# Attention scores as 64-row by 32-column tiles of the array, with another order of the opening loads

## The chip, the core and the metric

The kernel runs on one core of one Trainium2 chip. The metric is the device time of one execution in microseconds (us). TensorE is called PE here, its weight loads PEld, VectorE DVE, ScalarE ACT, GpSimd POOL and SyncE SP, as the profile names them.

## The reference

Attention with RMS-normalised queries and keys over 8 batches, 12 heads, 448 positions and 64 dimensions a head, followed by a feed-forward part on the 3584 tokens: two products with 768 by 1024 weights, multiplied with each other, then two more products without anything in between.

```
q_n, k_n = rmsnorm(q, g_q), rmsnorm(k, g_k)        # x / sqrt(mean(x*x) + 1e-6) * g
scores = matmul(q_n, k_n^T) / sqrt(64)
attn = softmax(scores)
x = (attn @ v) as 3584 x 768
h = (x @ w1) * (x @ w2) @ w3
out = h @ w_out
```

## The kernel before

**Staging.** The 96 (batch, head) pairs are worked on as NQ = 24 groups of HQ = 4 heads. The loop at L473 runs over the groups (and one round more), with four slots each (`sl`); t = 4 i + sl numbers the slots. In one slot the kernel issues, in this order for PE: the scores of two key blocks of a head pair (`qk_exp`, L226), one set of the products with v for the group before (`pv_set`, L248: first the row sums with a matrix of ones, then the two halves of the head dimension), then either units of a weight product (slots 1 to 13) or up to two units of the feed-forward part (`fill`), and then what is due of the preparation of later groups. The order is written out by hand, and each engine works through its own instructions in this order.

**Scores.** 448 positions are four blocks of NP = 112. For one key block, `qk_exp` issues two matmuls, one for each head of the pair (L235): head u lies on partitions 64 u to 64 u + 63 of `qkT`, so each matmul uses 64 rows of the array and all 112 columns, and streams the 448 queries. Both land in one PSUM tile `sc` (two banks, two such tiles in turn), and one ACT instruction takes the exponential of both (L244). A slot has two key blocks, four matmuls.

**Other PE work.** `pv_set` (L259) and the feed-forward part (`narrow`, L314) issue groups of four matmuls of 32 columns each, at column positions 0, 32, 64 and 96, over all rows (112 and 128). In slots 1 to 13 the product w3 times w_out is made once, so that the feed-forward part needs three products and not four: `w3_transpose` (L293, transposes of 128 by 128) and `w34_unit` (L301, matmuls of 128 by 128 streaming 384 columns). `w34q` at L443 orders these units: the second half of the output columns (nh = 1) follows the first by LAG = 4 chunks, and `W34_SLOTS` says how many units a slot takes. From slot 14 on, feed-forward units take that place.

**Preparation.** For each group, squares on ACT (L157), sums on DVE (L166), the factor 1/rms as `alpha` on ACT (L176, L177), the scaling on DVE (`prep_scale`, L188 to L201, with the product of both g vectors, `g_b`), then the transposition of the scaled q and k to `qkT`: for the groups below N_PE_T = 5 on PE (L220) with a copy by DVE (L223), for the others by a transposing DMA on SP's queue (L210). The tables PREP and SHIFT say in which slot before its use each part is issued.

**Opening.** POOL's queue first broadcasts g_q and g_k to 112 partitions (L401, L402). q and k of group 0 are loaded in two parts each, q on SP's queue and k on ACT's, then q and k of group 1 on SP's. A small POOL copy (L410, `gate`) reads the last part of k and so holds back POOL's weight loads behind it: both pieces of w_out's first column half (`load_wout(0, ...)`), four chunks of w3, v of group 0, both pieces of w_out's second half. Sixteen matmuls on zeros (`warm`) run at the start. The remaining loads are in the list `wq` (L432), four of which are issued in each slot: w3 chunks 4 to 7, v of groups 1 and 2, then w1 and w2. At L424 and L425 DVE multiplies the two g vectors and the factor 8 into `g_b`, between `alpha` and the first scaling.

Of the kernel before, what the change touches and what calls it, by code (L numbers as in the profile page):

```python
# [8 lines left out]
FP = mybir.dt.float32  # L9
BF = mybir.dt.bfloat16  # L10
MULT = mybir.AluOpType.mult
# [7 lines left out]
def kernel(  # L19
# [13 lines left out]
    nc = tc.nc  # L33

    B, H, S, D = q.shape
    NP = 112
    J = S // NP
    HQ = 4
# [4 lines left out]
    CF = DFF // 128  # L43
# [4 lines left out]
    const = ctx.enter_context(tc.tile_pool(name="const", bufs=1))  # L48
# [9 lines left out]

    big_pool = ctx.enter_context(tc.tile_pool(name="big", bufs=2))

    N_PE_T = 5
    N_SQ_ACT = 24
    W34_EV = "DA"
    LAG = 4
    SHIFT = [0, 0, 0, -1, -2, -3, -4]
    PREP_1 = {
        "sq0": -4, "red0": -4, "sq1": -4, "red1": -3, "alpha": -3,
# [11 lines left out]
    w_outs = const.tile([128, CF, DM], BF, name="w_outs")  # L79
    w3s = big_pool.tile([128, CF, DFF], BF, tag="big", name="w3s")  # L80
    w3T = big_pool.tile([128, CF, DFF], BF, tag="big", name="w3T")
    gq_b = const.tile([NP, D], FP, name="gq_b")
    gk_b = const.tile([NP, D], FP, name="gk_b")
    g_b = const.tile([NP, D], BF, name="g_b")
    ident = const.tile([128, 128], BF, name="ident")
    ones = const.tile([NP, HALF], BF, name="ones")
# [11 lines left out]
    def load_qk(i, split=1, k_eng=None):  # L98
        b, m = divmod(i, NQB)
        s = st[i]  # L100
        s["q"] = load_pool.tile([NP, HQ, J, D], FP, tag="q", name="q_sb")
        s["k"] = load_pool.tile([NP, HQ, J, D], FP, tag="k", name="k_sb")
        n = HQ // split
        for h0 in range(0, HQ, n):
            for t_sb, src, eng in (
                (s["q"], q, nc.sync),
                (s["k"], k, k_eng or nc.sync),
            ):
                eng.dma_start(
                    out=t_sb[:, h0 : h0 + n].rearrange("p h j d -> p h (j d)"),  # L110
                    in_=src[b, HQ * m + h0 : HQ * m + h0 + n].rearrange(
                        "h (p j) d -> p h (j d)", j=J
                    ),
                )

    def load_v(i):
        b, m = divmod(i, NQB)
        s = st[i]
        s["v"] = load_pool.tile([NP, HQ, J, D], BF, tag="v", name="v_sb", bufs=4)
        nc.gpsimd.dma_start(  # L120
            out=s["v"].rearrange("p h j d -> p h (j d)"),
            in_=v[b, HQ * m : HQ * (m + 1)].rearrange("h (p j) d -> p h (j d)", j=J),
        )
# [9 lines left out]
    def load_w3(c):  # L133
        nc.gpsimd.dma_start(
            out=w3s[:, c, :],
            in_=moe_w3.rearrange("(c p) f -> p c f", p=128)[:, c, :],
        )

    def load_wout(nh, c):
        nc.gpsimd.dma_start(  # L140
            out=w_outs[:, 4 * c : 4 * c + 4, nh * NH : (nh + 1) * NH],
            in_=moe_w_out.rearrange("(c p) n -> p c n", p=128)[
                :, 4 * c : 4 * c + 4, nh * NH : (nh + 1) * NH
            ],
        )


    def prep_sq(i, pr, on_act=False):
# [77 lines left out]
    def qk_exp(i, g):  # L226
        s = st[i]
        if g == 0:
            s["P"] = att_pool.tile([NP, HQ, J, S], BF, tag="P", name="P")
        pr, t = divmod(g, 2)  # L230
        qkT, P = s["qkT"], s["P"]
        for jk in (2 * t, 2 * t + 1):
            sc = sc_psum.tile([NP, 2, 512], FP, tag="sc", name="sc")
            for u in range(2):
                nc.tensor.matmul(  # L235
                    out=sc[:, u, 0:S],
                    lhsT=qkT[u * D : (u + 1) * D, pr, J + jk, :],
                    rhs=qkT[u * D : (u + 1) * D, pr, 0:J, :].rearrange(
                        "d j p -> d (j p)"
                    ),  # L240
                    start=True,
                    stop=True,
                )
            nc.scalar.activation(  # L244
                out=P[:, 2 * pr : 2 * pr + 2, jk, :], in_=sc[:, :, 0:S], func=AF.Exp
            )
# [151 lines left out]

    with tc.manual_schedule():

        nc.gpsimd.dma_start(out=gq_b, in_=g_q.unsqueeze(0).broadcast_to([NP, D]))  # L401
        nc.gpsimd.dma_start(out=gk_b, in_=g_k.unsqueeze(0).broadcast_to([NP, D]))  # L402
        nc.vector.memset(warm_t, 0.0)
        nc.vector.memset(eps_t, 64e-6)
        nc.vector.memset(ones, 1.0)
        load_qk(0, split=2, k_eng=nc.scalar)
        nc.scalar.preload_act_table_set("natural_log_exp_and_others")
        load_qk(1)
        make_identity(nc, ident)
        nc.gpsimd.tensor_copy(out=gate, in_=st[0]["k"][:, HQ - 1, 0, 0:1])  # L410
        load_wout(0, 0)
        load_wout(0, 1)
        for c in range(4):
            load_w3(c)
        load_v(0)
        load_wout(1, 0)
        load_wout(1, 1)
        warm(16)
        for pr in range(2):
            prep_sq(0, pr, on_act=True)  # L420
            prep_red(0, pr)
            prep_alpha(0, 2 * pr, 2 * pr + 2)
            if pr == 0:
                nc.vector.tensor_tensor(out=gq_b, in0=gq_b, in1=gk_b, op=MULT)  # L424
                nc.vector.tensor_scalar(  # L425
                    out=g_b, in0=gq_b, scalar1=8.0, scalar2=None, op0=MULT
                )
            prep_scale(0, pr, pe=True)
            if pr == 0:
                prep_pe_transpose(0, 0)  # L430

        wq = [lambda c=c: load_w3(c) for c in range(4, CF)]  # L432
        wq.insert(2, lambda: load_v(1))
        wq.append(lambda: load_v(2))
        for h in range(HQ):
            for half in range(2):
                for w, src in ((w1s, moe_w1), (w2s, moe_w2)):
                    wq.append(
                        lambda w=w, src=src, h=h, half=half: load_w12(w, src, h, half)
                    )  # L440
        wq.append(lambda: load_v(3))

        w34q = [lambda: w3_transpose(0), lambda: w3_transpose(1)]  # L443
        for fc in range(CF + LAG):
            if fc < CF:
                w34q.append(lambda fc=fc: w34_unit(fc, 0))
            if fc + 2 < CF:
                w34q.append(lambda fc=fc: w3_transpose(fc + 2))
            if fc >= LAG:
                w34q.append(lambda fc=fc: w34_unit(fc - LAG, 1))  # L450

        def prep_part(n, part):
            pe = n < N_PE_T
            if part[:2] == "sq":
                prep_sq(n, int(part[2]), on_act=n < N_SQ_ACT)
            elif part[:3] == "red":
                prep_red(n, int(part[3]))
            elif part == "alpha":
                prep_alpha(n)
            elif part[:2] == "sc":  # L460
                prep_scale(n, int(part[2]), pe=pe)
            elif pe:
                prep_pe_transpose(n, int(part[1]))


        agenda = {}
        for n in range(1, NQ):
            shift = SHIFT[min(n, len(SHIFT)) - 1]
            table = PREP_1 if n == 1 else PREP
            for part, rel in table.items():  # L470
                agenda.setdefault(max(0, 4 * n + rel + shift), []).append((n, part))

        for i in range(NQ + 1):  # L473
            for sl in range(4):
                t = 4 * i + sl
                mine = agenda.pop(t, [])
                for n, part in mine:
                    if part == "load":
                        load_qk(n)
                if i < NQ:  # L480
                    qk_exp(i, sl)
                if t == 0:
                    prep_pe_transpose(0, 1)
                seen = len(fillers)
                if i > 0 and sl < 3:
                    pv_set(i - 1, sl)
                fresh = fillers[seen:]
                if sl == 0 and 4 <= i + 1 < NQ:
                    load_v(i + 1)
                for _ in range(4):  # L490
                    if wq:
                        wq.pop(0)()
                if t in W34_SLOTS:
                    for _ in range(W34_SLOTS[t]):
                        if w34q:
                            w34q.pop(0)()
                elif not w34q:
                    left = (14 - t) % 12 + 1
                    old = len(fillers) - sum(1 for f in fillers if f in fresh)
                    fill(min(2, -(-old // left)))  # L500
                for n, part in mine:
                    if part[0] == "t":
                        prep_part(n, part)
                for n, part in mine:
                    if part[0] != "t" and part != "load":
                        prep_part(n, part)
        fill(len(fillers))
# [28 lines left out]
```

## Time and profile before

Six runs: median 391.97 us, from 391.19 to 393.34.

| | us |
|---|---|
| the profiled execution | 391.9 |
| its span, first to last instruction | 390.0 |
| score matmuls, L235, busy (384 of them, mean 378 ns) | 57.4 |
| their exponentials on ACT, L244, busy (192, mean 916 ns) | 165.4 |
| feed-forward matmuls pa, pb, po, L314, busy | 84.0, 83.7, 77.9 |
| products with v and row sums, L259, busy | 45.1, 22.6 |
| weight product, L301, busy | 24.0 |
| PE transposes of q and k, L220, busy (80, 10 sets of 8) | 7.0 |
| DVE waits for g_k | 3.0 |
| transposing DMAs, L210: 38, us to landing, least / median / most | 2.9 / 4.1 / 6.3 |

Busy times of matmuls have modelled ends and overlap each other; a mean of 378 ns for a matmul is its way through the array, while the next one has already started. The mean granted clock of PE is 0.982 of the full one; over the span's stretch from 10 to 20 us it was 0.57, from 20 to 30 us 0.75, and 1.00 from 30 us on. In the stretches from 10 to 60 us the DMA engines were busy all the time (a share above 1, as packets overlap); from 70 to 80 us the share was 0.49.

The first feed-forward matmul starts at 68.9 us, the last load of w1 and w2 was issued at 53.0, and the last stretch, from 356 us on, has feed-forward work alone.

### The profile page before, as it was taken

What the parts mean: (1) busy time and instruction counts of PE and PEld (TensorE: products, weight loads), DVE (VectorE), ACT (ScalarE), POOL (GpSimd) and SP (SyncE); (2) the same over time, 40 slices, a digit from 0 to 9 for tenths busy, and PEclk for the clock granted to TensorE, in tenths of its full rate; (3) what the DMA queues carried; (4) which work ended last, traced back from release to release, by engine and by line L of the source; (5) the groups of instructions that cost most, each with busy time, mean ns of one, the idle gap of its engine ahead of it and who ended that gap; (6) DMA issues with size and microseconds to landing.
All of it is one profiled execution on the core that took longest, in us unless ns stands there. A gap on an engine that the chain in (4) does not pass through costs nothing.

```text
span 390.0 us, 14802 instructions
## 1 busy us (share of the span) xinstructions
PE 372.7 (96%) x6688; PEld 193.1 (50%) x6688; DVE 242.4 (62%) x383; ACT 285.3 (73%) x467; POOL 35.4 (9%) x61
## 2 busy tenths in 40 slices
PE   5498999999999999999999999999999999999995
PEld 1154554544544455445544554445445555456563
DVE  1775766887767677567766766757776672234232
ACT  4568889998888885897898768888889857751210
POOL 5332440000000000000000000000000000000000
PEclk9579999999999999999999999999999999999999
DMA  8999999387895589675877489559854651003014
GB/s 188 229 238 237 207 227 188 61 156 140 200 206 87 117 167 211 121 164 92 192 173 155 78 222 208 73 110 198 207 91 122 119 141 27 3 12 114 2 26 140
DMA packets 78367, 55.08 MB, mean 141 GB/s; under 512 B 37824, under 2 KB 72160, under 8 KB 78304
## 3 DMA queue, kind: packets, MB, share of 16 engines
q1 hardware_dynamic: 61568, 41.30, 44.8%
q0 software_dynamic: 16256, 12.38, 22.6%
q8 instruction: 52, 0.85, 1.0%
q10 hardware_dynamic: 480, 0.46, 0.4%
q14 instruction: 11, 0.09, 0.1%
HBM read 46.72 MB, written 11.01 MB: 148 GB/s over the span
## 4 chain that ended last, share of the span: by engine, by line
PE 87%; DMA 8%; ACT 1%; DVE 1%; POOL 0%; issue 0%; ACTq 0%
PE pa L314 19%; PE po L314 19%; PE pb L314 19%; PE pv L259 15%; PE sc L235 12%; DMA w3s<-in_moe_w_dram 4%; PE wps L301 3%; DMA w_outs<-in_moe_w_out_dram 3%; DMA k_sb<-in_k_dram 1%; PE w3T_ps L293 1%; PE qkT_ps L220 0%; ACT P L244 0%; DVE qtmp L188 0%; ACT w34s L286 0%; DVE qks L201 0%; ACT sq L157 0%
## 5 line engine op out<-in xcount | busy, mean ns | idle before, releaser
L244 ACT ACTIVATE P<-sc 112x896 bf16<-112x896 f32 x192 | 165.4, 916 | 41.7 <-PE sc L235 41.7
L344 DVE TENSOR_TENSOR abT<-pb,a_sb 128x448 bf16<-128x448 f32 x64 | 40.0, 625 | 77.0 <-PE pb L314 56.6
L314 PE MATMUL pa<-xT,w1s 128*32 128x448 bf16 x1536 | 84.0, 353 | 0.0
L314 PE MATMUL pb<-xT,w2s 128*32 128x448 bf16 x1536 | 83.7, 352 | 0.0
L314 PE MATMUL po<-w34s,abT 128*32 128x384 bf16 x1792 | 77.9, 326 | 0.0
L166 DVE TENSOR_REDUCE ssq<-sq 112x16 f32<-112x1024 f32 x48 | 58.3, 1215 | 13.9 <-ACT sq L157 13.9
L314 PEld LDWEIGHTS <-abT 128*32 128x32 bf16 x1792 | 47.2, 97 | 27.7 <-issue 2.4
L235 PE MATMUL sc<-qkT 64*112 64x448 bf16 x384 | 57.4, 378 | 0.7 <-DVE qkT L223 0.7
L314 PEld LDWEIGHTS <-w2s 128*32 128x32 bf16 x1536 | 41.1, 97 | 31.5
L314 PEld LDWEIGHTS <-w1s 128*32 128x32 bf16 x1536 | 39.7, 96 | 34.1 <-issue 4.7
L331 ACT CAST a_sb<-pa 128x448 bf16<-128x448 f32 x64 | 34.0, 531 | 26.5 <-PE pa L314 26.5
L363 DVE COPY o_sb<-po 128x384 f32<-128x384 f32 x56 | 31.2, 557 | 31.5 <-PE po L314 31.5
L259 PE MATMUL pv<-P,v_sb 112*32 112x448 bf16 x768 | 45.1, 355 | 0.0
L120 POOL DMA_DIRECT2D v_sb<-in_v_dram x24 | 17.0, 708 | 238.2 <-PE pv L259 217.8
L188 DVE TENSOR_TENSOR qtmp<-q_sb,alpha 112x512 bf16<-112x512 f32 x48 | 32.8, 683 | 6.8 <-ACT alpha L177 6.8
L235 PEld LDWEIGHTS <-qkT 64*112 64x112 bf16 x384 | 17.4, 126 | 31.8 <-issue 29.4
L201 DVE TENSOR_TENSOR qks<-k_sb,alpha 112x512 bf16<-112x512 f32 x48 | 32.9, 685 | 0.0
L275 DVE TENSOR_TENSOR xT<-pv,r 128x448 bf16<-128x448 f32 x48 | 29.6, 618 | 3.2 <-PE pv L259 3.2
L157 ACT ACTIVATE sq<-q_sb 112x512 f32<-112x512 f32 x48 | 30.4, 634 | 1.5 <-DMA q_sb<-in_q_dram 1.5
L157 ACT ACTIVATE sq<-k_sb 112x512 f32<-112x512 f32 x48 | 30.0, 625 | 0.0
L259 PEld LDWEIGHTS <-v_sb 112*32 112x32 bf16 x768 | 16.2, 95 | 23.7 <-issue 15.6
L301 PE MATMUL wps<-w_outs,w3T 128*128 128x384 bf16 x128 | 24.0, 338 | 0.0
(36 smaller groups left out, 174.3 us busy)
## 6 DMA issues: line engine op xcount, KB each, us to landing
q_sb<-in_q_dram SPq DMA_DIRECT2D x23, 448.0 KB, 5.5
k_sb<-in_k_dram SPq DMA_DIRECT2D x23, 448.0 KB, 6.1
v_sb<-in_v_dram POOLq DMA_DIRECT2D x24, 224.0 KB, 4.8
out_dram<-o_sb SPq DMA_DIRECT2D x8, 336.0 KB, 3.9
out_dram<-o_sb SPq DMA_DIRECT2D x8, 288.0 KB, 3.6
w3s<-in_moe_w_dram POOLq DMA_DIRECT2D x8, 256.0 KB, 15.6
out_dram<-o_sb SPq DMA_DIRECT2D x8, 240.0 KB, 4.0
w_outs<-in_moe_w_out_dram POOLq DMA_DIRECT2D x4, 384.0 KB, 13.5
```

The source lines that it names most:

```text
L157: nc.scalar.activation(out=sq[:, t], in_=src[:, hs], func=AF.Square)
L166: nc.vector.tensor_reduce(out=s["ssq"][:, :, hs, :], in_=s.pop(("sq", pr)), axis=AX, op=ADD)
L188: nc.vector.tensor_tensor(out=qtmp.transpose([0, 2, 1, 3]), in0=s["q"][:, hs], in1=alpha[:, 0, hs].unsqueeze(3).broadcast_to([NP, 2, J, D] ...
L201: nc.vector.tensor_tensor(out=qks[:, 1].transpose([0, 2, 1, 3]), in0=s["k"][:, hs], in1=alpha[:, 1, hs].unsqueeze(3).broadcast_to([NP, 2, ...
L235: nc.tensor.matmul(out=sc[:, u, 0:S], lhsT=qkT[u * D : (u + 1) * D, pr, J + jk, :], rhs=qkT[u * D : (u + 1) * D, pr, 0:J, :].rearrange("d ...
L244: nc.scalar.activation(out=P[:, 2 * pr : 2 * pr + 2, jk, :], in_=sc[:, :, 0:S], func=AF.Exp)
L259: nc.tensor.matmul(out=ps[h * HALF : (h + 1) * HALF, :], lhsT=w, rhs=P[:, h, jk, :], start=(jk == 0), stop=(jk == J - 1), tile_position=(0 ...
L301: nc.tensor.matmul(out=ps[:, 0:NH], lhsT=w3T[:, gc, fc * 128 : (fc + 1) * 128], rhs=w_outs[:, gc, nh * NH : (nh + 1) * NH], start=(gc == 0 ...
L314: nc.tensor.matmul(out=ps[32 * h : 32 * h + 32, 0:n], lhsT=lhsT[:, 32 * h : 32 * h + 32], rhs=rhs, start=start, stop=stop, tile_position=( ...
L331: nc.scalar.copy(out=a_sb, in_=ps[:, 0:S])
L344: nc.vector.tensor_tensor(out=abT[bp][:, fi, odd * S : (odd + 1) * S], in0=ps[:, 0:S], in1=a_tiles.pop((b, fi)), op=MULT,)
L363: nc.vector.tensor_copy(out=o_sb[:, nh * NH : (nh + 1) * NH], in_=ps[:, 0:NH])
```

## The change

Each score matmul of 64 rows by 112 columns becomes four of 64 rows by 32 columns (the last one has 16), at row position 64 u and column position c0. A key block of a head pair is then eight matmuls, at eight different places of the array, which stream the same queries and write the same PSUM tile in strips of 32 partitions.

The opening is reordered. The g vectors are no longer broadcast by POOL's DMAs: each is loaded as one row of 64 on ACT's queue, behind the k loads; DVE multiplies both rows and the factor 8 into `gp_row` on one partition, one matmul with a row of ones spreads it over 112 partitions, and DVE copies that from PSUM to `g_b`. The `gate` copy now reads the first part of q and not the last part of k. POOL's loads follow in the order of LOADS_0 and then LOADS_1: w3 chunk 4 and v of group 0 come earlier, w_out's second half comes later. LAG is 8 and not 4, so the units of w_out's second half all follow those of the first. N_PE_T is 3 and not 5: groups 3 and 4 are transposed by DMA. QK1_AT = -1 leaves the load of group 1 where it was.

```diff
-    N_PE_T = 5
+    N_PE_T = 3
-    LAG = 4
+    LAG = 8
+    LOADS_0 = ["o0", "w0", "w1", "w2", "v0", "w3", "w4"]
+    LOADS_1 = ["w5", "v1", "w6", "w7", "o1", "v2"]
+    GATE = ("q", 0)
+    QK1_AT = -1
...
+    def load_any(x):
+        kind, a = x[0], int(x[1])
+        if kind == "o":
+            load_wout(a, 0)
+            load_wout(a, 1)
+        elif kind == "w":
+            load_w3(a)
+        else:
+            load_v(a)
...
             for u in range(2):
-                nc.tensor.matmul(
-                    out=sc[:, u, 0:S],
-                    lhsT=qkT[u * D : (u + 1) * D, pr, J + jk, :],
-                    rhs=qkT[u * D : (u + 1) * D, pr, 0:J, :].rearrange(
-                        "d j p -> d (j p)"
-                    ),
-                    start=True,
-                    stop=True,
-                )
+                for c0 in range(0, NP, 32):
+                    c1 = min(c0 + 32, NP)
+                    nc.tensor.matmul(
+                        out=sc[c0:c1, u, 0:S],
+                        lhsT=qkT[u * D : (u + 1) * D, pr, J + jk, c0:c1],
+                        rhs=qkT[u * D : (u + 1) * D, pr, 0:J, :].rearrange(
+                            "d j p -> d (j p)"
+                        ),
+                        start=True,
+                        stop=True,
+                        tile_position=(u * D, c0),
+                    )
...
-        nc.gpsimd.dma_start(out=gq_b, in_=g_q.unsqueeze(0).broadcast_to([NP, D]))
-        nc.gpsimd.dma_start(out=gk_b, in_=g_k.unsqueeze(0).broadcast_to([NP, D]))
...
+        nc.vector.memset(ones_row, 1.0)
         load_qk(0, split=2, k_eng=nc.scalar)
+        nc.scalar.dma_start(out=g_row[:, 0], in_=g_q.unsqueeze(0))
+        nc.scalar.dma_start(out=g_row[:, 1], in_=g_k.unsqueeze(0))
         nc.scalar.preload_act_table_set("natural_log_exp_and_others")
-        load_qk(1)
+        if QK1_AT < 0:
+            load_qk(1)
         make_identity(nc, ident)
-        nc.gpsimd.tensor_copy(out=gate, in_=st[0]["k"][:, HQ - 1, 0, 0:1])
-        load_wout(0, 0)
-        load_wout(0, 1)
-        for c in range(4):
-            load_w3(c)
-        load_v(0)
-        load_wout(1, 0)
-        load_wout(1, 1)
+        nc.gpsimd.tensor_copy(out=gate, in_=st[0][GATE[0]][:, GATE[1], 0, 0:1])
+        for x in LOADS_0:
+            load_any(x)
...
             if pr == 0:
-                nc.vector.tensor_tensor(out=gq_b, in0=gq_b, in1=gk_b, op=MULT)
-                nc.vector.tensor_scalar(
-                    out=g_b, in0=gq_b, scalar1=8.0, scalar2=None, op0=MULT
-                )
+                nc.vector.scalar_tensor_tensor(
+                    out=gp_row, in0=g_row[:, 0], scalar=8.0, in1=g_row[:, 1],
+                    op0=MULT, op1=MULT,
+                )
+                g_ps = mm_psum.tile([NP, D], FP, tag="mm", name="g_ps")
+                nc.tensor.matmul(
+                    out=g_ps, lhsT=ones_row, rhs=gp_row, start=True, stop=True
+                )
+                nc.vector.tensor_copy(out=g_b, in_=g_ps)
...
-        wq = [lambda c=c: load_w3(c) for c in range(4, CF)]
-        wq.insert(2, lambda: load_v(1))
-        wq.append(lambda: load_v(2))
+        wq = [lambda x=x: load_any(x) for x in LOADS_1]
```

More of the change, by code (lines that the diff above doesn't have):

```diff
@@ L81 @@
     w3T = big_pool.tile([128, CF, DFF], BF, tag="big", name="w3T")
-    gq_b = const.tile([NP, D], FP, name="gq_b")
-    gk_b = const.tile([NP, D], FP, name="gk_b")
+    g_row = const.tile([1, 2, D], FP, name="g_row")
+    gp_row = const.tile([1, D], BF, name="gp_row")
+    ones_row = const.tile([1, NP], BF, name="ones_row")
     g_b = const.tile([NP, D], BF, name="g_b")
@@ L475 @@
                 t = 4 * i + sl
+                if t == QK1_AT:
+                    load_qk(1)
                 mine = agenda.pop(t, [])
```

## The prediction

> **What bounds the kernel now.** I read the page's first part, then the chain of waits, then PE's timeline, then the waits.
>
> ```profile
> PE 372.7 (96%) x6688; PEld 193.1 (50%) x6688; DVE 242.4 (62%) x383; ACT 285.3 (73%) x467; POOL 35.4 (9%) x61
> ```
>
> PE is busy 96% of the span, and the chain that ended last is 87% PE; so the question is what PE's microseconds consist of. The chain of waits in one steady stretch (start us, us, what):
>
> ```profile
> 119.50 0.87 PE pv L259 x16
> 120.38 1.14 PE pa L314 x24
> 121.51 1.14 PE pb L314 x24
> 122.65 0.52 PE sc L235 x4
> 123.16 1.25 PE pa L314 x24
> ```
>
> A group of four column-tiled FFN matmuls costs 1.14 / 6 = 0.19 us, which is one 448-column stream (eight untiled 384-column wps matmuls take 1.30 in the same chain: 0.1625 x 448 / 384 = 0.19). Four score matmuls are two pairs; each pair already runs as one (two 64-row halves side by side), so 2 x 0.19 = 0.38 us would do. They take 0.52: entering the scores costs 0.14. The next piece pays again: pa 1.25 where it is 1.14 elsewhere, and pv 0.87 where 4 x 0.19 = 0.76: leaving costs 0.11. PE's weight loads show why:
>
> ```profile
> 121.15 1.05 PEld L314 LDWEIGHTS <-w2s 128*32 128x32 bf16 x24
> 122.58 0.18 PEld L235 LDWEIGHTS <-qkT 64*112 64x112 bf16 x4 [0.37 <-issue]
> 123.09 0.88 PEld L314 LDWEIGHTS <-w1s 128*32 128x32 bf16 x24 [0.34 <-issue]
> 124.05 1.05 PEld L314 LDWEIGHTS <-w2s 128*32 128x32 bf16 x24
> ```
>
> From pa to pb the load of w2s (124.05) starts before the stream of pa is over; at both edges of the scores the load waits 0.34 to 0.37 us for nothing that the profile names. The reader is to see a bubble at each change of tile shape, not a wait for data. So the change cannot gain from running "eight at a time": the stream is as long as before. It can gain at the two edges.
>
> **The edges: is a change of rows alone free?** All scores become 64-row by 32-column tiles between 128-row (or 112-row) by 32-column work. What the trace has of shape changes, in the stretch where the weight fold runs at 128 columns:
>
> ```profile
> 40.04 0.52 PE sc L235 x4
> 40.55 0.55 PE w3T_ps L293 x8
> ...
> 44.33 1.41 PE wps L301 x8
> 45.73 0.45 PE w3T_ps L293 x8
> ```
>
> Here 128 by 128 to scores costs the same 0.14 (0.52), scores to 128 by 128 costs 0.10 (0.55 against 0.45), and pv (32 columns, all rows) to wps costs 0.11 (1.41 against 1.30 for the same eight at 41.11). So a change of columns alone costs the full price. A change of 112 to 128 rows at 32 columns (pv to pa at 120.38) costs nothing. A change of rows alone is shown only by 128 by 128 to scores, and that one is not pure, as the by-form groups of weight loads show:
>
> ```profile
> L314 PEld LDWEIGHTS <-w1s 128*32 128x32 bf16 x1536 | 39.7, 96 | 34.1 <-issue 4.7
> L235 PEld LDWEIGHTS <-qkT 64*112 64x112 bf16 x384 | 17.4, 126 | 31.8 <-issue 29.4
> L301 PEld LDWEIGHTS <-w3T 128*128 128x128 bf16 x128 | 12.2, 101 | 9.5 <-issue 3.2
> ```
>
> A load of 112 columns takes 126 ns and one of 128 columns 101, so the 128-column load is of another kind, and that step changes the kind of load along with the rows. The bounds of the edge after the change are therefore 0 (as pv to pa) and about 0.11 to 0.14 us (as today; the shorter 32-column load, 96 against 126 ns, could take 0.03 off the entry). I take 0: the neighbours will share the column width and the kind of load, as pv and pa do. It is little better than even.
>
> One page speaks against this. The Trainium skill, "TensorEngine Tiling (Array Packing)", under Key Properties, says that changing the tiling mode drains the engine, and lists 64 by 32 as another mode than 128 by 32; by it the edges stay and the time would be the 388 of the first rival below, and not 370. The trace agrees for columns, and leaves rows alone open.
>
> **The sum,** against the profiled execution: 391.9 us, its span 390.0 and 1.9 around it; the median of the six runs is 391.97, so the sum can be read against either.
>
> Entries: along the timeline 80 of the 96 score groups follow 32-column work: 80 x 0.14 = 11.2 us. Sixteen follow 128-column work and keep their edge. Exits: 69 groups are followed by pv and 21 by FFN: 90 x 0.11 = 9.9 us.
>
> The opening.
>
> ```profile
> PE w3T_ps L293 <- DMA w3s<-in_moe_w_dram: 3.0, 2, 1.6
> DVE gq_b L424 <- DMA gk_b<-in_g_k_dram: 3.0, 1, 3.0
> ```
>
> DVE waits 3.0 us for the broadcast of g_k, which lands at 9.8; alpha was ready at 7.5. Now two rows of 256 B go on ACT's queue behind the two k loads (landed 6.3): 2 x 0.45 us of issue ahead of the table load, which ends near 3.9 instead of 3.0, still ahead of the first square at 4.52. Then one DVE operation, one small matmul and a PSUM copy, about 0.2, 0.3 and 0.2 us by the rows of gq_b, a cold transpose and g_b: the first scaling moves from 10.3 to 8 to 8.5 (not at all, if the rows land at 9.8 too). Queued behind the new waits stand only the scaling on DVE and the transposes on PE that need it anyway. That by itself gains nothing: PE next waits 1.6 us for the first w3 chunk, landed 19.9. That chunk moves with the gate, opened by q's first half (4.5) and not by k's second (6.35). As the DMA engines are 84% busy in the first 10 us, I take 1.0 of these 1.8. PE's second wait, 1.38 us for w3 chunk 4 at 34.44, goes, since that chunk now stands ahead of both late w_out loads. Together 2.4, between 0 and 3.0. LAG 8 only swaps weight-fold units of equal size within the same slots, and lets those w_out loads be late: nothing.
>
> N_PE_T 3 removes four sets of eight PE transposes, of the query and key groups 3 and 4: three cost 0.40 in the chain, the last one 1.25 with its waits for DVE (67.0 to 68.3): 2.4 us off PE. Their four DVE copies go too. Four DMA transposes come onto SP's queue (1.24 us to issue, 2.9 to 6.3 us to land, median 4.1); behind them on SP stand the loads of later q and k, not needed for two slots or more. The tight one is the first of group 3: its input is done at 53.1, its scores start at 58.3, 5.2 us later, in a stretch where DMA is saturated and a k load took 15.6 us to land. A wait of 0 to 5 us; I take +1.0.
>
> ACT takes some back.
>
> ```profile
> 60.00:80.00 20.00, 19.38 (x292) 9.74 (x293) 15.66 (x25) 19.65 (x36) 0.70 (x1) 1.00 0.69 135
> ```
>
> The fourth busy time is ACT's: 19.65 of 20 us, and 17.95 in the 20 us before, so ACT can give up 2.4 us from 40 to 80. PE would shed about 4.0 there (2.4 transposes, four entries, nine exits): 1.6 is given back. Later ACT runs 34.7 of 40 us; twelve slots less 12 x 0.25 = 3.0 us make that 93%, and I add 1.0 for slots with two squares. Sum: 391.9 - 11.2 - 9.9 - 2.4 - 2.4 + 1.0 + 2.6 = 369.6, say 370 us. If one edge of the two stays, 380; own range 364 to 381.
>
> **Rivals.** First, the row change drains as it does today: only the load's 0.03 and a later start of the eighth tile differ (80 x 0 to 0.03, less than 2.4 us), with the opening's 2.4 and some 1.2 of the transposes left over beside ACT: 391.9 - 1.2 - 2.4 - 1.2 + 1.0 = 388, from 384 to 390. For it: 128 by 128 to scores costs what every change costs. Against it: that step changes the load as well.
>
> Second, slower: issue becomes the limit. A pair of scores becomes 16 PE instructions instead of 4. The densest sustained stretch of the trace, 64 po matmuls in 2.60 us, is 40.6 ns for a matmul with its load. If that were PE's pace, eight take 325 ns instead of 190: 192 x 0.135 = +25.9 us, and with the edges kept 391.9 + 25.9 - 3.6 = 414. It decides from 209 ns a group of eight if the edges stay (3.6 / 192), from about 300 if they go. Against it: po is itself bound by its 384-column stream, and starts within a group of four lie about 4 ns apart; a slot of 80 matmuls needs 3.2 us even at that pace, less than today's 3.66, so instructions queued ahead could cover it.
>
> Third, it does nothing: edges stay, and late DMA transposes (up to 5 us, once) and ACT eat the opening's gain: 391 to 393.
>
> **How the numbers follow.** Edges go, wholly or half: 0.50. Edges stay: 0.32. Issue limit or a worse opening: 0.13. Nothing: 0.05. A measurement of this kernel tells about 0.3% (1.2 us) from no change. Faster: 0.50 and nearly all of 0.32, less for a late transpose, 0.77; same 0.08; slower 0.15. The time is 370, and the range reaches over the first rival: 364 to 390.
>
> **What would show it.** In the profile after: the chain's sc piece (then x16) at 0.38 to 0.40 and not 0.50; pv after it at 0.76; the score loads starting before the stream ahead of them ends, with no issue gap; edges left only against 128-column work. No w3T wait at the fourth chunk; scaling near 8 us. Wrong it is if the score loads still show a gap of 0.3 us, or if a group of eight spans clearly more than 0.19 us; ACT near 100% past 80 us would mean that I undercounted ACT.

## The result

The changed kernel takes 393.96 us (median of 21 runs, 392.57 to 395.46), the kernel before 391.94 (42 runs): a ratio of 1.005, with a 95% interval from 1.0037 to 1.0064. It is a little slower, where 370 us was forecast. The profiled execution took 393.8 us, its span is 392.0.

The page's first part after:

```profile
PE 373.5 (95%) x7809; PEld 188.0 (48%) x7809; DVE 240.6 (61%) x380; ACT 285.5 (73%) x467; POOL 34.1 (9%) x59
```

PE issues 1121 matmuls more (1152 of the scores, less 32 transposes, and one for the g vectors) and is as busy as before. The chain of waits in a steady stretch (start us, us, what):

```profile
121.91 0.50 PE sc L252 x10
122.41 0.87 PE pv L277 x16
123.28 1.14 PE pa L332 x24
...
125.56 0.50 PE sc L252 x11
126.06 1.25 PE pa L332 x24
```

(The chain lists ten or eleven of the sixteen score matmuls; the others start beside them.) Scores take 0.50 us where they took 0.52, and leaving them costs what it did: pv 0.87, pa 1.25. PE's weight loads of the same stretch:

```profile
121.84 0.14 PEld L252 LDWEIGHTS <-qkT 64*32 64x32 bf16 x16 [0.37 <-issue]
122.34 0.50 PEld L277 LDWEIGHTS <-v_sb 112*32 112x32 bf16 x16 [0.36 <-issue]
122.92 1.05 PEld L332 LDWEIGHTS <-w1s 128*32 128x32 bf16 x24
```

The loads of the scores and of pv behind them still wait for the array to empty, 0.36 to 0.37 us; those of pa behind pv do not. Both edges are where they were.

The second finding is at slot 12. The chain from 46 to 66 us:

```profile
46.76 0.50 PE sc L252 x10
47.25 0.87 PE pv L277 x16
48.12 1.49 PE wps L319 x9
49.61 9.38 DMA qkT<-qks
58.99 0.04 issue
59.03 0.94 PE sc L252 x8
59.98 1.62 PE pv L277 x15
61.59 4.13 PE wps L319 x16
65.72 0.50 PE sc L252 x12
```

The transposing DMA of group 3 is issued at 49.6 us and lands 9.4 us later, where 2.9 to 6.3 was seen before. PE has nothing to do from 54.0 to 59.0. What follows is slow too: pv takes 1.62 us and not 0.87, sixteen wps 4.13 and not 2.71. In these two stretches of the span (PE's busy time is the first of the five engines', the granted clock stands after the fifth, then the DMA share):

```profile
50.00:60.00 10.00, 5.00 (x58) 2.15 (x59) 4.14 (x6) 5.30 (x11) 1.40 (x2) 0.88 1.24 201
60.00:70.00 10.00, 9.86 (x104) 4.07 (x105) 3.18 (x6) 7.01 (x14) 0.00 (x0) 0.78 0.48 98
```

The granted clock falls to a half from 57.6 to 64.5 us, and the DMA engines are full in the first stretch. Against the timeline of before, the first score matmul of slot 11 starts at 50.76 us and not at 54.69 (3.9 us ahead), that of slot 13 at 65.65 and not at 62.40 (3.3 behind): the wait and the cold clock take 7.2 us. The 80 slots after that win back a little: 2.0 us behind at the end.

So the opening's part of the gain came, the edges' part did not, and the transposing DMA cost more than the opening brought.

### The profile page after: what moved, and what is told of

Same layout as the page of the kernel before. It is cut to its first block, busy times and chain, and to the rows that moved or that the text cites. A ratio compares the mean times of both kernels' runs of the same rounds, so it can differ in the third digit from the quotient of the medians.

```text
span 392.0 us, 17054 instructions
## 1 busy us (share of the span) xinstructions
PE 373.5 (95%) x7809; PEld 188.0 (48%) x7809; DVE 240.6 (61%) x380; ACT 285.5 (73%) x467; POOL 34.1 (9%) x59
## 4 chain that ended last, share of the span: by engine, by line
PE 89%; DMA 6%; ACT 3%; POOL 0%; DVE 0%; issue 0%
PE pa L332 19%; PE po L332 19%; PE pb L332 19%; PE pv L277 15%; PE sc L252 12%; PE wps L319 4%; DMA w3s<-in_moe_w_dram 3%; DMA qkT<-qks 2%; ACT P L262 1%; PE w3T_ps L311 1%; DMA q_sb<-in_q_dram 1%; ACT sq L172 1%; PE qkT_ps L235 0%; POOL w_outs L145 0%; ACT w34s L304 0%; ACT r L289 0%
## 5 line engine op out<-in xcount | busy, mean ns | idle before, releaser
L252 PE MATMUL sc<-qkT 64*32 64x448 bf16 (+1 forms) x1536 | 56.5, 362 | 7.4 <-DMA qkT<-qks 5.0
L252 PEld LDWEIGHTS <-qkT 64*32 64x32 bf16 (+1 forms) x1536 | 13.3, 87 | 40.3 <-issue 33.1
L319 PE MATMUL wps<-w_outs,w3T 128*128 128x384 bf16 x128 | 25.5, 353 | 0.0
```

The lines of the kernel that those rows point to most:

```text
L252: nc.tensor.matmul(out=sc[c0:c1, u, 0:S], lhsT=qkT[u * D : (u + 1) * D, pr, J + jk, c0:c1], rhs=qkT[u * D : (u + 1) * D, pr, 0:J, :].rearr ...
L319: nc.tensor.matmul(out=ps[:, 0:NH], lhsT=w3T[:, gc, fc * 128 : (fc + 1) * 128], rhs=w_outs[:, gc, nh * NH : (nh + 1) * NH], start=(gc == 0 ...
```

## The experiments

The runs are called e1 to e12, as in brackets below. The kernel before ran beside each of three sets of runs, with medians of 391.28 (e1 to e4), 392.17 (e5 to e8) and 391.81 us (e9 to e12); ratios are against that of the same set. "After" in the diffs is the changed kernel.

### The transposing DMA of groups 3 and 4

**After with groups 3 and 4 on PE (e1).**

```diff
-    N_PE_T = 3
+    N_PE_T = 5
```

> The changed kernel with N_PE_T = 5 again, all else kept. Theory (late DMA transpose): the profile after loses 5.0 us at slot 12 to a transposing DMA and about 2.6 us more to the cold clock behind it; with groups 3 and 4 on PE again the wait is gone, at about 2.4 us of PE work, so 387 to 389 us, ratio to before 0.988 to 0.993, no DMA wait before any score matmul. Rival (the tiled scores cost the time elsewhere): 392 to 394.

Measured: 389.25 us, ratio 0.9945 (0.9927 to 0.9964). Slot 12 starts at 54.92 us, no score matmul waits for a DMA, and the clock stays up from 23 us on. 389.25 is just above the range that was expected; part of what stands in the way, a stop of PE, is shown below, under the instructions.

**Before with N_PE_T = 3 alone (e3).**

```diff
-    N_PE_T = 5
+    N_PE_T = 3
```

> The kernel before with nothing changed but N_PE_T = 3. Theory: the transposing DMA of group 3 is late here too, 4 to 5 us of wait and 1 to 3 us of cold clock less 1 to 2 us of transposes saved: 395 to 399 us. Rival (it is late only because the opening's loads were reordered): 390 to 392.

Measured: 399.19 us, ratio 1.0194 (1.0175 to 1.0213): 7.9 us from this one number. The chain shows the same piece in the old opening:

```profile
53.59 9.40 DMA qkT<-qks
62.99 0.04 issue
63.03 0.99 PE sc L235 x4
...
65.64 4.33 PE wps L301 x16
```

It is not the new order of the loads that makes the transpose late.

**After without the loads of w2 (e6).**

```diff
-                for w, src in ((w1s, moe_w1), (w2s, moe_w2)):
+                for w, src in ((w1s, moe_w1),):
...
-                ps, S, w2s[:, c, fi * 128 : (fi + 1) * 128], xT[b][:, c, :],
+                ps, S, w1s[:, c, fi * 128 : (fi + 1) * 128], xT[b][:, c, :],
```

> The changed kernel without the eight loads of w2 (w1 is used for both products, so that factor of the feed-forward part is left out). Theory (the transposing DMA is late because POOL's weight loads fill the DMA engines): that backlog ends about 8 us sooner, the transposes of group 3 land in 3 to 6 us and not 9.4, PE's wait at slot 12 is 0 to 1.5 us, the clock stays up: 386 to 389 us. Rival (these transposes are slow by themselves or by SP's queue): 9 us to landing and the 5 us wait as before, 393 to 394.

Measured: 386.79 us, ratio 0.9856 (0.9799 to 0.9913). The transpose is issued at 49.9 us, as in the changed kernel, but is off the chain: PE goes on and ACT becomes the limit.

```profile
48.44 2.72 PE wps L319 x16
51.16 0.02 issue
51.18 0.48 ACT w34s L304
```

With eight weight loads less, the same instruction from the same queue is in time. Its own landing is not in the trace, but the scores of slot 12 start at 54.28 us without a wait for it, 4.4 us after its issue, and no transpose whose landing is recorded takes more than 6.8 us. The last load of w1 lands at 48.5 us here, before the transpose is issued, and the last of w2 at 55.7 in the changed kernel. So it was late because weight loads still filled the DMA engines when it was issued.

**After with group 3 prepared one slot earlier (e7).**

```diff
-    SHIFT = [0, 0, 0, -1, -2, -3, -4]
+    SHIFT = [0, 0, -1, -1, -2, -3, -4]
```

> The changed kernel with the preparation of group 3 one slot earlier (SHIFT for n = 3 is -1). Theory: the transpose is issued some 3.5 us earlier, but into full DMA engines, and is used at the same slot: the wait falls from 5.0 to 1 to 2.5 us and the cold stretch shortens, 388 to 391 us. Rival (a transpose lands only when the weight loads are done, near 59 us, whenever it is issued): the wait stays 4 to 5 us, 393 to 394.

Measured: 393.66 us (392.52 to 396.42), ratio 1.0038 (1.0007 to 1.0068). My expectation fell; the time is the rival's:

```profile
44.84 2.13 PE wps L319 x13
46.97 14.99 DMA qkT<-qks
61.96 0.04 issue
62.00 0.94 PE sc L252 x10
```

Issued 2.6 us earlier, the transpose took 15.0 us instead of 9.4 and landed later than in the changed kernel, and PE waited 7.2 us for it. This trace is of the longest of the ten executions, 396.42 us, so 15.0 us is not the usual case; but the median is level with the changed kernel, and nothing was won. Nor does the transpose simply wait for the weight loads: the last two that were issued ahead of it took 6.8 and 7.0 us to land, the four behind it 11.3 to 12.1, so that the last landed at 62.2 us and not at 55.7. Issued into full engines, the transpose and the loads behind it are late together.

**After with group 4 alone by DMA (e8).**

```diff
-    N_PE_T = 3
+    N_PE_T = 4
```

> The changed kernel with N_PE_T = 4: group 3 by PE, group 4 by DMA. Theory: only group 3 was late; group 4's transposes go out near 65 us, when the weight loads are done, and PE sheds one or two sets of transposes: at or below e1, 386 to 388.5 us. Rival (group 4 is late too): a DMA wait at slot 16, 389 to 392.

Measured: 388.55 us, ratio 0.9895 (0.985 to 0.994). Group 4's transposes are issued at 61.4 and 64.0 us, when the last load of w1 and w2 has landed; the first lands in 3.1 us, the second in 7.1, and no score matmul waits for either. So group 4 by DMA does no harm, and group 3 by DMA cost all the rest.

### The edges of the scores

**Before with the tiled scores alone (e2).** The edit is the score part of the change, nothing else.

> The kernel before with nothing changed but the scores as eight tiles. Theory (the change of rows drains as before, only the shorter weight load is saved): score pieces of 0.50 us in the chain and not 0.52, 80 to 96 x 0.015 to 0.02 = 1.2 to 1.9 us faster, 390.0 to 390.8 us. Rival (eight issues cost something that the chain of after does not show): slower than 392. The forecast on record would have been 371.

Measured: 392.10 us (390.01 to 393.25), ratio 1.001 (0.9987 to 1.0033). The profiled execution, at 390.01, has score pieces of 0.50 us and is what was expected; the median is not, and the interval leaves both signs open. What is settled is that the forecast 20 us are not there.

**Scores over all 128 rows (e5).** Two groups of four, as pv and the feed-forward part are issued, so that no matmul of a steady slot differs in the height or width of its tile.

```diff
-                        lhsT=qkT[u * D : (u + 1) * D, pr, J + jk, c0:c1],
-                        rhs=qkT[u * D : (u + 1) * D, pr, 0:J, :].rearrange(
+                        lhsT=qkT[:, pr, J + jk, c0:c1],
+                        rhs=qkT[:, pr, 0:J, :].rearrange(
...
-                        tile_position=(u * D, c0),
+                        tile_position=(0, c0),
```

> As e1_after_pe5, but every score matmul takes all 128 rows (both heads of the pair summed, so the scores are not the reference's), in 32-column tiles: eight matmuls in two groups of four. The stream doubles: 4 x 0.19 = 0.76 us a slot. Theory (what drains is the change of row height, 128 to 64): both edges next to 32-column work are gone, the score piece is 0.76, pv behind it 0.76 and pa 1.14, and the loads start ahead of the stream's end; 96 x 0.38 less about 19 = 13 to 19 us above e1. Rival (the edge belongs to the score matmuls, by what they wait for): the piece is 0.87 or more, pv 0.87, 33 to 38 us above e1.

Measured: 404.86 us in the profiled execution, 15.2 above the 389.70 of the profiled execution of e1. The chain, and the weight loads:

```profile
120.27 0.76 PE sc L252 x10
121.03 0.76 PE pv L277 x12
121.79 1.14 PE pa L332 x14
122.93 1.14 PE pb L332 x13
124.06 0.76 PE sc L252 x9
124.82 1.14 PE pa L332 x12
```

```profile
119.88 0.71 PEld L252 LDWEIGHTS <-qkT 128*32 128x32 bf16 x16
120.63 0.71 PEld L277 LDWEIGHTS <-v_sb 112*32 112x32 bf16 x16
121.39 1.09 PEld L332 LDWEIGHTS <-w1s 128*32 128x32 bf16 x24
```

(The chain lists only some of the matmuls of a piece.) Every piece is its bare stream: four groups 0.76, pv 0.76, pa 1.14, and no load waits. The semaphores, the tiles and the order are those of e1; the row height alone differs. So the drain is that of the change from 128 rows to 64 and back, at equal columns. It is of no use as a version: the second stream costs 0.26 us a slot more than the tiled scores and their entry, to save 0.11.

**Tiles of 64 by 64 (e11).**

```diff
-                for c0 in range(0, NP, 32):
-                    c1 = min(c0 + 32, NP)
+                for c0 in range(0, NP, 64):
+                    c1 = min(c0 + 64, NP)
```

(and N_PE_T = 4)

> As e10, with score tiles of 64 by 64: eight matmuls a slot and not sixteen. The columns change too at the edges. Theory (any change of shape drains alike, and only the first weight load's length counts): score pieces near 0.51 us in the chain, between the 0.50 of 32 columns and the 0.52 of 112, and the time within 1 us of e10. Rival (a change of both rows and columns costs more than one of rows): pieces over 0.53.

Measured: 387.76 us (386.47 to 388.74), ratio 0.9883 (0.9857 to 0.9908), the fastest of the study.

```profile
124.33 1.14 PE pb L332 x24
125.47 0.50 PE sc L252 x6
125.97 0.87 PE pv L277 x16
```

The pieces are as short as with 32 columns, 0.50 us and not between that and 0.52, at half the matmuls; changing the columns as well costs nothing more. That the first load's length alone counts is thereby wrong. In the traces (medians over the score groups of slots 30 to 89 whose first load waits) that load takes 123 ns with 112 columns, 103 with 64 and 89 with 32; but the last tile of a key block starts 3, 10 and 20 ns after its first. The last score matmul of a slot so starts 238, 222 and 222 ns after the first load.

**The weight fold's second half in 32-column tiles (e12).**

```diff
+            if nh == 1:
+                narrow(
+                    ps, NH, w3T[:, gc, fc * 128 : (fc + 1) * 128],
+                    w_outs[:, gc, nh * NH : (nh + 1) * NH], gc == 0, gc == CF - 1,
+                )
+                continue
```

(in `w34_unit`, with the old scores and N_PE_T = 4)

> As e9, with the second half of the weight fold (nh = 1) as 32-column tiles like pv. Theory (equal row height and equal column width: no edge): wps behind pv loses its 0.11 us at four places, pv to wps loads start ahead of the stream's end; at most 0.5 us in all, and nothing where ACT is the limit there: 0 to 0.5 us below e9. Rival (matmuls over 128 rows drain behind 112-row ones when weights change): no change of the edge.

Measured: 389.66 us, ratio 0.9938 (0.9911 to 0.9966), against 390.10 and 0.9945 of e9 below: no difference that can be told. The edge itself is gone:

```profile
46.87 0.87 PE pv L274 x16
47.74 2.60 PE wps L335 x64
```

The narrow fold (now 64 matmuls) takes 2.60 us behind pv, where the wide one took 2.71. pv has 112 rows and the fold 128, so these count as one height. The edge has partly moved: eight PE transposes behind the narrow fold take 0.50 us, where behind the wide one in e9 they take 0.40.

### The opening, and the instructions

**The opening alone (e4):** after with the old score matmuls and N_PE_T = 5.

> The changed kernel with the old score matmuls and N_PE_T = 5: the opening's loads, the gate, the g vectors and LAG 8 alone. Theory: PE stood 3.5 us ahead of before at slot 10 in the profile after, of which some is given back to ACT, so 388 to 390 us. Rival (the gain is all given back by slot 16, where ACT is full): 391.5 to 392.5.

Measured: 388.89 us, ratio 0.9942 (0.9929 to 0.9956): 2.4 us faster. In the profiled executions slot 11 starts 3.5 us ahead of before, slot 16 3.5 and the end 3.0: little is given back to ACT.

**Old scores (e9) and tiled scores (e10) side by side,** both with the new opening and N_PE_T = 4; e10 is the same kernel as e8.

> The new opening and N_PE_T = 4 with the old score matmuls. Theory A (tiles save 0.017 us a slot, as the chain shows): 1.3 to 1.8 us above e10 in the same call, 389 to 390.5. Theory B (what the tiles save, PE's instruction fetch takes back in some executions): equal to e10 within 0.5 us.

> e8_after_pe4 once more, beside e9: 387 to 388.5 us. Theory A: 1.3 to 1.8 us below e9, with as narrow a spread. Theory B: level with e9, with executions 1 to 3 us apart.

Measured: old scores 390.10 us, ratio 0.9945 (0.9924 to 0.9966); tiles 389.23 (386.69 to 389.92), ratio 0.9909 (0.9878 to 0.9939). The intervals overlap, so neither theory is settled by the times. Nor do the other pairs of one set show a gain from the tiles: e1 with them took 389.25 us and e4 without them 388.89, e2 with them 392.10 and before 391.28. The traces say more. From the first score matmul of slot 16 to that of slot 95, the timeline gives 274.69 us in each of before, e3, e9 and e12 and 274.76 in e4, all with the old scores. With tiles it gives 273.37 in after and e2 and 273.38 in e8, the 1.3 us that 0.017 a slot make, but 273.8 and 273.9 in e7 and e6, 275.56 in e1 and 275.72 in e10. In e10's timeline of PE:

```profile
151.97 0.74 PE L332 MATMUL pa<-xT,w1s 128*32 128x448 bf16 x12
153.63 0.75 PE L332 MATMUL pa<-xT,w1s 128*32 128x448 bf16 x12 [0.93 <-issue]
```

and in e1's:

```profile
145.38 1.31 PE L332 MATMUL po<-w34s,abT 128*32 128x384 bf16 x28
147.78 1.65 PE L332 MATMUL po<-w34s,abT 128*32 128x384 bf16 x36 [1.08 <-issue]
```

PE stops in the middle of a group, for about 1 us, and waits for nothing that the profile names. e1 has a second one of 0.49 us at 153.97, and e5, with as many score matmuls, two of 0.47 and 1.60 us: stops in three of the eight traces with sixteen score matmuls a slot. No trace with the old scores has such a stop in these 80 slots, nor has the one with 64 by 64 tiles. The queue that the page calls "instruction" carries 61 packets of 16 KB in e1, 55 in e11 and 52 before, one for every 256 or 257 matmuls and weight loads of PE in each. In e1 one is fetched at 135.6 us and the next only at 145.4, where the median distance is 5.8. That PE runs out of instructions there is a guess that no run took apart, and these rows are weak support: in e10 the longest distance nearby, from 135.7 to 144.5 us, ends 8 us before the stop, and before has one of 9.5 us without a stop. The cause of the stops stays open.

## Why the prediction was wrong

**The step that failed** is the bound chosen for the edges: "The bounds of the edge after the change are therefore 0 (as pv to pa) and about 0.11 to 0.14 us ... I take 0". It measured 0.12 on the way in (0.50 less 0.38) and 0.11 on the way out. Of the 11.2 us of entries 1.3 came, what the shorter first load leaves after the later start of the last tile; of the 9.9 of exits nothing. The trace had the row: 128 by 128 to scores, a change of rows next to the full width, cost the same 0.14 as the entry from 32-column work. I set it aside because that step also changes the kind of weight load, which nothing showed to cost a drain. e5 closes this: at equal rows and columns both edges vanish. The page that was weighed there, the Trainium skill's "TensorEngine Tiling (Array Packing)", Key Properties and the list of configurations above it, was right in its plain form: 64 by 32 is another mode than 128 by 32, and the change between them drains, at 0.12 and 0.11 us here. The first rival had this mechanism.

**The late transpose** is the second term that failed: it was seen, bounded at 0 to 5 us and taken at 1.0. The wait was 5.0, the bound's end, and the bound left out what comes behind: 2.6 us of cold clock (pv 1.62 less 0.87, wps 4.13 less 2.71, scores 0.94 less 0.50). I took the value near the steady median of 4.1 us, though the nearest row in time, a k load issued at 42.6 in the same full stretch, had taken 15.6. With 7.6 in the place of 1.0, the first rival's 388 becomes 394.6, against 393.96 measured; the third rival, "late DMA transposes ... eat the opening's gain", named the outcome and had 0.05. The forecast's own sum comes near as well: 369.6, with 19.8 us of edges that stayed and 6.6 more for the transpose, makes 396.0, or 393.4 without the 2.6 charged for ACT at a pace that never came.

**The opening** came out as forecast in the medians, 2.4 us in e4, but not by its parts, so that the agreement is partly luck. The first w3 chunk is used at 17.5 us in e4 and not at 19.95, and slot 3 starts 2.3 us ahead, where 1.0 was taken; the granted clock also rises 2.1 us earlier, at 23.0 us and not at 25.1. The fourth-chunk wait of 1.4 us is gone, as forecast. That makes 3.5 us at slot 11 and 3.0 at the end of the profiled execution. The scaling starts at 8.15 us in after and 8.63 in e4, and not at 10.3 (8 to 8.5 forecast).

**The transposes on PE,** 2.4 us less for two groups, brought nothing that can be told for group 4. From slot 11 to slot 17 e8 takes 20.08 us and e1 20.16; with the old scores e9 takes 20.17 and e4 20.23. What PE sheds it spends waiting for ACT, most of it at slot 15; e8's list of waits has this row, where e1 has none for the exponentials:

```profile
PE sc L252 <- ACT P L262: 1.5, 2, 1.1
```

By the medians e8 stands 0.7 us below e1, but in another set of runs, and e10, the same kernel again, took 389.23 us, level with e1's 389.25. What group 3's transposes would save is not shown, as the wait covers it.

**ACT's share** was not put to the test at the forecast pace, but its limit near slot 15 is real at the measured one: 1.5 to 1.6 us of waits in after, e6 and e8.

**Issue as a limit**, the second rival: the second group of eight starts 0.20 us after the first (median of the same slots), so the price of 325 ns is not there. What some runs have instead are stops of 0.5 to 1.6 us, enough to hide a gain of 1.3.

**LAG 8** was costed at nothing and not tried alone.

## What to carry to other kernels

In these runs every change of tile shape on TensorE that was priced cost 0.10 to 0.14 us, whichever side of the tile changed (112 rows and 128 counted as the same), and no edge was left where rows and columns both matched the neighbours'; so count the edges, not the tiles. A transfer that takes over from an engine is priced by what the same stretch's transfers took to land (15.6 us for a k load here), not by the run's median (4.1 us), and a long wait of TensorE is charged with the cold clock behind it, 2.6 us for a wait of 5.0 here. Where a bound rests on a row that is set aside, try the sum with that row first.

## What the runs showed of the hardware

A transposing DMA issued while weight loads fill the DMA engines took 9.4 us to land in the changed kernel and in e3, and 15.0 in one long execution of e7, issued 2.6 us earlier; four weight loads issued behind that one took 11.3 to 12.1 us, where the two ahead of it took 6.8 and 7.0. With the weight loads over, in e8, no recorded one took more than 7.1. A wait of 5.0 us on TensorE brought the granted clock to one half from 57.6 to 64.5 us, 2.6 us more of lost time; in e3 the clock fell likewise, from 62.1 to 68.9. Weight loads of 32, 48 and 64 columns took 89, 98 and 105 ns at 64 rows (after and e11); one of 112 took 126 (before). The edge between 128 by 32 and 64 by 32 tiles cost 0.12 us in and 0.11 out, and nothing in e5, where the scores had 128 rows.
